# Gates by seven products in 42 of 48 quads, first products copied from bank to bank, and engine orders from a list scheduler

## The chip, the cores and the metric

The kernel runs on one core of one Trainium2 chip. The metric is the time of one execution on the device in microseconds, as the median of several runs. Before the change it is 533.65 us (three runs, 532.7 to 536.5). The profile shows one execution of 529.3 us from its first to its last instruction.

The core has five engines, each with its own instruction stream: TensorE (PE; PEld is its loading of weights) multiplies matrices and writes to PSUM, a memory of eight banks of 128 x 512 fp32; VectorE (DVE) works element by element; ScalarE (ACT) applies functions and copies; GpSimd (POOL) and SyncE (SP) here mostly start DMA transfers. [...]

## The reference

Attention in which keys and values are first projected from 1024 positions to 64, and then a feed-forward layer with a sigmoid gate. Inputs and output are fp32; the kernel computes its products in bf16.

```python
# attention: q, k, v are (8, 8, 1024, 64), E and F are (64, 1024)
k_proj = np.einsum('ks,bhsd->bhkd', E, k)
v_proj = np.einsum('ks,bhsd->bhkd', F, v)
scores = np.matmul(q, k_proj.transpose(0, 1, 3, 2)) / 8
attn = np.exp(scores - scores.max(-1, keepdims=True))
attn = attn / (attn.sum(-1, keepdims=True) + 1e-09)
x = np.matmul(attn, v_proj)            # then (8192, 512): heads side by side

# feed-forward: w_gate, w_val are (512, 1536), w_out is (1536, 512)
gate = 1.0 / (1.0 + np.exp(-(x @ w_gate)))
out = (gate * (x @ w_val)) @ w_out
```

## The kernel before

**The unit of work.** The 8 batches have 1024 rows of x each. Half a batch (512 rows) is a block, so there are 16 blocks. The hidden width of 1536 is cut into 12 pieces of 128. A quad is one third of a block: two pieces of the lower half of the hidden width and two of the upper half, for 512 rows. There are 3 quads a block, 6 a batch, 48 in all. Block 0 (three quads) is computed plainly while weights arrive; from quad 3 on the values use Strassen's scheme in Winograd's form: 7 products of half size in place of 8, with sums of operands beforehand and sums of products afterwards. The output product uses the same scheme from block 1 on. `vT`, `wT` hold sums of weights, `xS`, `hS` sums of the left operands.

**Gates**, one step for one piece: four matmuls of 512 columns into a PSUM bank, then a tanh on ScalarE (the sigmoid is written as a tanh of half the argument). `K` is the quad, `n` is 0 to 3.

```python
def g_step(K, n):
    ...
    bk = FF.take()
    for i in range(NI):                      # NI = 4
        mm_one(blk, m, i, "G", bk)           # 128x128 weights, 512 columns
    act(sg[:, n % 2, :], bank[bk][:, :], ..., func=AF.Tanh, scale=0.5)
    FF.append(bk)
```

**Values**, one quad: seven products of four matmuls of 256 columns, in two banks `a` and `c`. The first product is needed in two sums. It is copied to SBUF (`v_snap`) and added there to the second product (`v_add`). Products 2 and 6 and so on go on adding to bank `a`, which ScalarE copies at two points. `hidden` multiplies value and gate.

```python
def p1():
    held_v["a"] = a = FF.take()
    v_product(blk, q, a, "A11", "B11", start=True)
    v_snap(0, a)                                         # ACT: bank a -> SBUF

def p26():
    a = held_v["a"]
    held_v["c"] = c = FF.take()
    v_product(blk, q, c, "A12", "B21", start=True, stop=True)
    v_add(0, c)                                          # DVE: bank c + SBUF
    v_product(blk, q, a, "S2", "T2")
    v_snap(1, a)
    hidden(K, 0, 0, vsnap[0][:, :], [("vsnap", 0)])      # DVE: (tanh + 1) * value

def p57():  # S1 T1 into c, S3 T3 into a; v_snap(2, a); v_add(2, c)
def p4():   # A22 T4 into a; hidden from bank a; hidden from vsnap 2
def p3():   # S4 B22 into c; v_add(1, c); hidden from vsnap 1
```

**Output**, one block: `first_products` and `last_products` make seven products of 12 matmuls of 256 columns, with copies `keep_snap` (ACT) and sums `add_snap` (DVE) in the same manner. `s_sums` makes the sums of the left operands in VectorE, some split into a part of 4 and a part of 2 pieces.

**Attention** of batch b + 1 runs beside the feed-forward work of batch b. K and V are projected (16 matmuls), scores go through Exp, sums of the exponentials (denominators) are made by matmuls with a selection matrix, and the mixed values are copied unscaled to `xu`. The reciprocals are gathered by small DMAs and spread to all partitions by GpSimd; then VectorE multiplies:

```python
def spread(rnd):
    for j in range(4):
        n = 4 * rnd + j
        for c, parts in ((1, P), (0, 64)):
            pool(lambda e, ...: e.partition_broadcast(rb[0:parts, n, :], rrow[...], channels=parts), ...)

def x_half(r, g, bks):                                   # ACT: PSUM -> xu
    act(xu[:, n, :], bank[bks[g]][:, :], [], [("xu", n)], b=bks[g])

def mul(r, g, bk=None):                                  # DVE: xT = xu * rb
    y = rb[:, n, :] if bk is None else bank[bk][:, :]
    dve(lambda e: e.tensor_tensor(xT[...], xu[:, n, :]..., y..., ALU.mult), ...)
```

**The order** of each engine is written by hand: the quad's pieces are put in a row (`todo`), and other work is hung on positions in it.

```python
def quad_pieces(K, more):
    p1, p26, p57, p4, p3 = v_pieces(K)
    return [p1, lambda: g_step(K, 1), p26, lambda: g_step(K, 2), p57,
            lambda: g_step(K, 3), p4, lambda: g_step(K + 1, 0)], p3
...
on(2, 0, lambda: first_products(o0, first))              # quad 2, position 0
on(2, 2, lambda: last_products(o0))
on(ks, 0, n["scores"]); on(ks + 1, 0, n["mixed"]); on(3, 0, n["outputs"])
```

Four banks (`FF`) serve gates and values, four (`AA`) outputs and attention; a bank is taken from the head of its list and given back at the end.

Of the kernel before, what the change touches and what calls it, by code (L numbers as in the profile page):

```python
# [7 lines left out]
ALU = mybir.AluOpType  # L8
# [18 lines left out]

class Plan:
# [3 lines left out]
    def __init__(self):  # L32
        self.ops = []
        self.writers = {}
        self.readers = {}
        self.dma_count = {}

    def add(self, eng, fn, r=(), w=(), x=(), dma=None):
# [80 lines left out]
def bass_linformer_attn__then__ffn_glu_sigmoid_kernel(  # L119
# [18 lines left out]
    with contextlib.ExitStack() as es:  # L138
# [6 lines left out]
        wT = sbuf("wT", [P, 4, NF // 2, 256], BF16)  # L145
# [3 lines left out]
        def within(shape, dtype):  # L149
# [38 lines left out]
        rb = (  # L188
            KVs[:, :, :, :].rearrange("p w h c -> p (w h c)").bitcast(FP32)
            .rearrange("p (n c) -> p n c", n=8)  # L190
        )
# [6 lines left out]
        rrow = (  # L198
            eT[:, :, :].rearrange("p n c -> p (n c)").bitcast(FP32)
            .rearrange("p (i c) -> p i c", i=4)  # L200
        )
# [11 lines left out]
        snap = [EF[:, 0:512], EF[:, 512:1024], sbuf("snap2", [P, 512], FP32)[:, :]]  # L213
        vsnap = [sbuf(f"vsnap{i}", [P, 512], FP32) for i in range(3)]
        xS = [sbuf(f"xS{i}", [P, 4, 2, 256], BF16) for i in range(2)]
# [50 lines left out]
        def act(o, i, r, w, b=None, func=AF.Copy, scale=1.0):  # L266
            x = [] if b is None else [("bank", b)]
            return add("ACT", lambda e: e.activation(o, i, func, scale=scale), r=r, w=w, x=x)  # L268

        def dve(fn, r, w, b=None):  # L270
            x = [] if b is None else [("bank", b)]
            return add("DVE", fn, r=r, w=w, x=x)
# [8 lines left out]
        def load(o, i, w, sem, r=()):  # L281
            add("POOL", lambda e: e.dma_start(o, i), r=r, w=w, dma=sem)  # L282
# [487 lines left out]
        def keep_kd(bk):  # L770
# [8 lines left out]
                b=bk,  # L779
            )  # L780
# [11 lines left out]
        def vd_one(bk, g):  # L792
# [6 lines left out]
            )  # L799

        def attention(b):
# [44 lines left out]
            def rec(c):  # L846
# [5 lines left out]
                    b=bk,  # L852
                )
# [54 lines left out]
            def gather():  # L908
                for m in (0, 1, 4, 5, 2, 3, 6, 7):
                    half_, i = m // 4, m % 4  # L910
                    add(
                        "SP",
                        lambda e, m=m, i=i, half_=half_: e.dma_start(
                            rrow[::32, i, 256 * half_ : 256 * half_ + 256], rden[m::32, :]
                        ),
                        r=[("rden", c, R) for c in range(2) for R in range(2)],
                        w=[("rrow", i, half_)] + [("eT", 2 * i + x) for x in range(2)],
                        dma=f"rrow{m}",
                    )

            def spread(rnd):
                for j in range(4):
                    n = 4 * rnd + j
                    for c, parts in ((1, P), (0, 64)):
                        pool(
                            lambda e, n=n, i=2 * rnd + c, j=j, parts=parts: e.partition_broadcast(  # L926
                                rb[0:parts, n, :], rrow[32 * j : 32 * j + 1, i, :], channels=parts
                            ),
                            r=[("rrow", 2 * rnd + c, x) for x in range(2)]
                            + [("eT", 4 * rnd + 2 * c + x) for x in range(2)]  # L930
                            + ["q7"],
                            w=[("rb", n), ("KV", n // 4, n % 4 // 2)],
                        )

# [19 lines left out]
            def mul(r, g, bk=None):  # L954
                n = 2 * r + g
                y = rb[:, n, :] if bk is None else bank[bk][:, :]
# [7 lines left out]
                    [("xu", n)]  # L964
# [90 lines left out]
            def keep_kv(n):  # L1055
                if "kv" not in held:
                    return
# [770 lines left out]
```

The softmax here doesn't subtract the row's maximum and nothing guards it: scores larger than these inputs give would overflow.

## Time and profile before

| | busy us | share of 529.3 us | instructions |
|---|---|---|---|
| TensorE, matmuls | 515.5 | 97% | 4110 |
| TensorE, weight loads | 350.8 | 66% | 4173 |
| VectorE | 416.3 | 79% | 681 |
| ScalarE | 307.2 | 58% | 551 |
| GpSimd | 133.4 | 25% | 148 |

Busy shares say how full an engine is on average over the whole span, not what it waits for. Matmul times in the profile include the pipeline, so successive ones overlap: the mean of one 512-column gate matmul is 379 ns in the groups, though they start closer together than that; starts in the timeline give the true spacing. Some matmul records are missing (707 of 768 of the gate matmuls are there).

The costliest groups outside TensorE on the page (line, engine, operation, out<-in, shape, count | busy us, mean ns | idle time before, and what ended most of it):

```profile
L926 POOL PARTITION_BROADCAST KVs<-eT x96 | 96.8, 1035 | 243.5 <-PE pF L264 190.7
L268 ACT ACTIVATE sig<-pF 128x512 f32<-128x512 f32 x192 | 115.4, 601 | 49.3 <-PE pF L264 47.3
L1476 DVE TENSOR_TENSOR vsnap<-pF,vsnap 128x512 f32<-128x512 f32 x135 | 93.0, 689 | 39.7 <-PE pF L264 29.5
L958 DVE TENSOR_TENSOR xT<-xu,KVs 128x512 bf16<-128x512 f32 x48 | 47.4, 1023 | 1.2 <-POOL KVs L926 0.7
```

The names are those of the buffers: `pF` and `pA` are PSUM banks, `sig` a gate, `vsnap` a value's partial sum, `rb` lies in `KVs` and `rrow` in `eT`. ScalarE and VectorE idle mostly until TensorE has finished a product.

### The profile page before, as it was taken

What the parts mean: (1) busy time and instruction counts of PE and PEld (TensorE: products, weight loads), DVE (VectorE), ACT (ScalarE), POOL (GpSimd) and SP (SyncE); (2) the same over time, 40 slices, a digit from 0 to 9 for tenths busy, and PEclk for the clock granted to TensorE, in tenths of its full rate; (3) what the DMA queues carried; (4) which work ended last, traced back from release to release, by engine and by line L of the source; (5) the groups of instructions that cost most, each with busy time, mean ns of one, the idle gap of its engine ahead of it and who ended that gap; (6) DMA issues with size and microseconds to landing.
All of it is one profiled execution on the core that took longest, in us unless ns stands there. A gap on an engine that the chain in (4) does not pass through costs nothing.

```text
span 529.3 us, 10415 instructions
## 1 busy us (share of the span) xinstructions
PE 515.5 (97%) x4110; PEld 350.8 (66%) x4173; DVE 416.3 (79%) x681; ACT 307.2 (58%) x551; POOL 133.4 (25%) x148
## 2 busy tenths in 40 slices
PE   5999999999999999999999999999999999999997
PEld 4545646656857667585766767576685867677676
DVE  4549786788987788877988779877888788997855
ACT  2565753688385564946468474764838564554541
POOL 9310200106700085001920048100650009200000
PEclk9999999999999999999999999999999999999999
DMA  9999999994393255911589223962620020202022
GB/s 167 199 199 202 155 213 195 184 171 89 35 230 60 82 91 84 231 53 38 90 157 162 80 40 57 213 105 80 88 86 1 0 83 3 80 1 79 1 81 80
DMA packets 77154, 56.18 MB, mean 106 GB/s; under 512 B 34801, under 2 KB 69297, under 8 KB 77105
## 3 DMA queue, kind: packets, MB, share of 16 engines
q0 software_dynamic: 33984, 29.89, 36.6%
q1 hardware_dynamic: 43120, 25.63, 19.4%
q8 instruction: 32, 0.52, 0.4%
q14 instruction: 18, 0.14, 0.1%
HBM read 60.29 MB, written 16.78 MB: 146 GB/s over the span
## 4 chain that ended last, share of the span: by engine, by line
PE 90%; DMA 7%; issue 1%; POOL 1%; DVE 0%; ACT 0%; POOLq 0%
PE pF L264 59%; PE pA L264 31%; DMA wO<-in_moe_w_out_dram 2%; DMA qT<-Qb 2%; DMA KVs<-in_v_dram 2%; POOL KVs L282 0%; POOL Qb L282 0%; DVE rden L639 0%; DVE vsnap L1476 0%; ACT vsnap L268 0%; DVE ost L1338 0%; POOL quad L356 0%; POOLq L102 0%; POOLq L1813 0%
## 5 line engine op out<-in xcount | busy, mean ns | idle before, releaser
L264 PE MATMUL pF<-xT,wG 128*128 128x512 bf16 x707 | 186.8, 379 | 3.8 <-DMA wG<-in_moe_w_gate_dram 0.2
L926 POOL PARTITION_BROADCAST KVs<-eT x96 | 96.8, 1035 | 243.5 <-PE pF L264 190.7
L268 ACT ACTIVATE sig<-pF 128x512 f32<-128x512 f32 x192 | 115.4, 601 | 49.3 <-PE pF L264 47.3
L1476 DVE TENSOR_TENSOR vsnap<-pF,vsnap 128x512 f32<-128x512 f32 x135 | 93.0, 689 | 39.7 <-PE pF L264 29.5
L264 PEld LDWEIGHTS pF<-xT,wG 128*128 128x128 bf16 x768 | 74.2, 98 | 54.5 <-issue 1.7
L268 ACT ACTIVATE vsnap<-pF 128x512 f32<-128x512 f32 x135 | 80.7, 598 | 46.9 <-PE pF L264 42.4
L1457 DVE SCALAR_TENSOR_TENSOR hT<-sig,vsnap 128x512 bf16<-128x512 f32 x135 | 93.5, 693 | 6.2
L264 PE MATMUL pF<-xT,wV 128*128 128x256 bf16 (+1 forms) x408 | 66.9, 286 | 0.0
L264 PE MATMUL pA<-wO,hT 128*128 128x256 bf16 x534 | 63.4, 273 | 0.0
L264 PEld LDWEIGHTS pA<-wO,hT 128*128 128x128 bf16 x534 | 52.1, 98 | 6.6 <-DVE ost L1267 0.3
L264 PE MATMUL pF<-xS,wV 128*128 128x256 bf16 x360 | 54.1, 273 | 0.3
L264 PEld LDWEIGHTS pF<-xT,wV 128*128 128x128 bf16 x408 | 38.2, 98 | 23.9 <-issue 5.7
L264 PE MATMUL pF<-xS,vT 128*128 128x256 bf16 x360 | 54.0, 273 | 0.0
L264 PEld LDWEIGHTS pF<-xS,wV 128*128 128x128 bf16 x360 | 34.3, 98 | 25.6 <-DVE vsnap L1476 5.0
L958 DVE TENSOR_TENSOR xT<-xu,KVs 128x512 bf16<-128x512 f32 x48 | 47.4, 1023 | 1.2 <-POOL KVs L926 0.7
L268 ACT ACTIVATE EF<-pA 128x512 f32<-128x512 f32 x30 | 17.9, 597 | 46.9 <-PE pA L264 46.9
L264 PE MATMUL pA<-wT,hT 128*128 128x256 bf16 x360 | 44.2, 273 | 0.0
L264 PE MATMUL pA<-wT,hS 128*128 128x256 bf16 x360 | 41.7, 273 | 0.0
L264 PEld LDWEIGHTS pA<-wT,hT 128*128 128x128 bf16 x360 | 35.1, 98 | 7.4 <-ACT snap L268 0.3
L264 PEld LDWEIGHTS pA<-wT,hS 128*128 128x128 bf16 x360 | 35.1, 98 | 4.3 <-issue 0.2
L264 PEld LDWEIGHTS pF<-xS,vT 128*128 128x128 bf16 x360 | 35.2, 98 | 4.1
L1267 DVE SCALAR_TENSOR_TENSOR ost<-pA,EF 128x512 f32<-128x512 f32 x29 | 20.0, 688 | 19.8 <-PE pA L264 19.7
(113 smaller groups left out, 487.6 us busy)
## 6 DMA issues: line engine op xcount, KB each, us to landing
out_dram<-ost SPq DMA_DIRECT2D x60, 256.0 KB, 2.4
Qb<-in_q_dram POOLq DMA_DIRECT2D x7, 1024.0 KB, 20.5
KVs<-in_k_dram POOLq DMA_DIRECT2D x7, 1024.0 KB, 12.0
KVs<-in_v_dram POOLq DMA_DIRECT2D x7, 1024.0 KB, 16.2
wO<-in_moe_w_out_dram POOLq DMA_DIRECT2D x1, 1536.0 KB, 12.3
wG<-in_moe_w_gate_dram POOLq DMA_DIRECT2D x5, 256.0 KB, 17.9
wV<-in_moe_w_val_dram POOLq DMA_DIRECT2D x5, 256.0 KB, 18.5
KVs<-in_k_dram POOLq DMA_DIRECT2D x2, 512.0 KB, 7.8
```

Source lines behind the costliest of these rows:

```text
L264: return add("PE", lambda e: e.matmul(o, lhsT, rhs, **kw), r=r, x=[("bank", b)])
L268: return add("ACT", lambda e: e.activation(o, i, func, scale=scale), r=r, w=w, x=x)
L926: lambda e, n=n, i=2 * rnd + c, j=j, parts=parts: e.partition_broadcast(rb[0:parts, n, :], rrow[32 * j : 32 * j + 1, i, :], channels=parts),
L958: lambda e: e.tensor_tensor(xT[s][:, r, :, 256 * g : 256 * g + 256], xu[:, n, :].rearrange("p (f c) -> p f c", f=2), y.rearrange("p (f c) ...
L1267: lambda e: e.scalar_tensor_tensor(o, bank[bk][:, :].rearrange("p (j c) -> p j c", j=2), 0.5, snap[n].rearrange("p (j c) -> p j c", j=2), ...
L1457: lambda e: e.scalar_tensor_tensor(o, sg[:, :, cc], 1.0, x.rearrange("p (j c) -> p j c", j=2), ALU.add, ALU.mult,),
L1476: lambda e: e.tensor_tensor(o, bank[bk][:, :], o, ALU.add),
```

## The change

Three things change from batch 1 (quad 6) on; batch 0 keeps its way.

1. **Gates by seven products too.** 42 of 48 quads compute x @ w_gate as the values are computed: seven products of four 256-column matmuls (`g_chain`), in two banks, with `gT` for the sums of weights, made once by `gt_sums`. This is to spare one product in eight.
2. **The first product is copied from PSUM bank to PSUM bank** (`seed`). The second product then adds to it in the bank, and its addition on VectorE goes away. Values, gates and outputs all use it.
3. **The order of each engine comes from a list scheduler** (`arranged`), run when the program is built: tasks with assumed durations (`COST`), dependencies and target times (`goal`, with `PACE = 9.9` us a quad); an engine takes, among the tasks that are ready, the most urgent. Banks are fixed: two each for gates, values and outputs, two more for attention.

To make room in SBUF some buffers shrink. And the reciprocals go to DRAM and come back as broadcast loads into `xu` (`rd`, `rb`); VectorE multiplies straight from PSUM (`scaled`), so the copy to `xu` and the GpSimd broadcasts go. The third sum of x rows replaces A21 in place, and the output's sums are made for six pieces at once.

The diff, cut to its core:

```diff
+COST = {"PE": (0.0, 0.22), "ACT": (0.52, 0.12), "DVE": (0.63, 0.12), "SP": (0.1, 0.0), "POOL": (0.85, 0.0)}
+def arranged(tasks, free):
+    ...   # dependencies from the keys that tasks read and write; rank from goals
+        for e, some in ready.items():
+            first = max(now[e], min(t.at for t in some))
+            pick = min((t for t in some if t.at <= first + 1e-9), key=lambda t: (t.rank, t.n))
...
-        wT = sbuf("wT", [P, 4, NF // 2, 256], BF16)
+        wT = sbuf("wT", [P, 3, NF // 2, 256], BF16)
+        gT = sbuf("gT", [P, 3, 2, DFF // 2], BF16)
...
+        def seed(a, c):
+            add("ACT", lambda e: e.activation(bank[c][:, :], bank[a][:, :], AF.Copy, scale=1.0),
+                r=[("bank", c)], x=[("bank", a), ("bank", c)])
...
             def p1():
-                held_v["a"] = a = FF.take()
+                held_v["a"], held_v["c"] = a, c = FF.two()
                 v_product(blk, q, a, "A11", "B11", start=True)
-                v_snap(0, a)
+                seed(a, c)
             def p26():
-                v_product(blk, q, c, "A12", "B21", start=True, stop=True)
-                v_add(0, c)
+                v_product(blk, q, c, "A12", "B21", stop=True)
                 v_product(blk, q, a, "S2", "T2")
...
+        def g_chain(K, a, c, goals):
+            x_product(K, a, "A11", "B11", g0, True, True)
+            seed(a, c)
+            x_product(K, a, "S2", "T2", g1, True)
+            act(o12, bank[a][:, :], [], [k12], b=a)
+            x_product(K, c, "A12", "B21", g1 + 0.1, True)
+            tanh(o, bank[c][:, :], [], [k], b=c)
+            x_product(K, a, "S3", "T3", g2, True)
+            act(o22, bank[a][:, :], [], [k22], b=a)
+            x_product(K, c, "S1", "T1", g2 + 0.1, True, True)
+            plus_bank(o22, k22, c)
+            tanh(o22, o22, [k22], [k22])
+            x_product(K, a, "A22", "T4", g3, True)
+            tanh(o, bank[a][:, :], [], [k], b=a)
+            x_product(K, c, "S4", "B22", g4, True)
+            plus_bank(o12, k12, c)
+            tanh(o12, o12, [k12], [k12])
...      # v_chain: the same products for the values; o_chain: for the output
-            def gather(): ...      # 8 small DMAs
-            def spread(rnd): ...   # 8 partition_broadcast on GpSimd, twice
+            def spread():
+                add("SP", lambda e: e.dma_start(rd_v[b], rden[:, :]), ..., t=2.8)
+                for rnd in range(2):
+                    for c in range(2):
+                        for h in range(2):
+                            ...    # src = one row of rd_v for 64 partitions, 256 KB in SBUF
+                            add("SP", lambda e, ...: e.dma_start(rb[64 * c : 64 * c + 64, :, h, rnd, :], src), ..., t=4.0)
+            def scaled(r, g, bk):
+                dve(lambda e: e.tensor_tensor(xT[...], bank[bk][:, :]..., rb[:, j, :, rnd, :], ALU.mult), ...)
...
-            for u in range(6): ...  # todo, at, on(...): the order by hand
+        PACE = 9.9
+        GA, GC, VA, VC, OA, OC, XA, XB = A0, F0, A1, F1, A2, F2, A3, F3
+        for b in range(1, B):
+            for u in range(6):
+                K = 6 * b + u; t0 = when(K)
+                if u == 0: n["sc_visit"](t0 - 1.0, (0, 1), (GA, GC, XA, XB))
+                if u == 1: n["sc_visit"](t0 - 1.0, (2, 3), (GA, GC, XA, XB)); n["den_visit"](t0 + 6.0, XA)
+                if u == 3: n["xo_visit"](t0 - 1.0, (0, 1), (GA, GC, XA, XB))
+                if u == 4: n["xo_visit"](t0 - 1.0, (2, 3), (GA, GC, XA, XB)); ...   # and K, V of b + 2
+                g_chain(K, GA, GC, [t0 + PACE * x for x in (0.0, 0.2, 0.4, 0.6, 0.8)])
+                v_chain(K, VA, VC, [t0 + PACE * x for x in (0.55, 0.75, 0.95, 1.15, 1.35)])
+                if K % 3 == 2: ...  # o_chain(blk, OA, OC, ...), at the end final_chain
+        for t in arranged(tasks, {}):
+            for eng, fn, r, w, x, dma in t.calls:
+                add(eng, fn, r=r, w=w, x=x, dma=dma)
```

## The prediction

> **What bounds the kernel now.** I read the page first: busy shares, then the chain that ended last. A busy TensorE alone proves little, because its matmuls overlap in the records; the chain says whether anything else ever ends last.
>
> ```profile
> PE 515.5 (97%) x4110; PEld 350.8 (66%) x4173; DVE 416.3 (79%) x681; ACT 307.2 (58%) x551; POOL 133.4 (25%) x148
> PE 90%; DMA 7%; issue 1%; POOL 1%; DVE 0%; ACT 0%; POOLq 0%
> ```
>
> 90% of the chain is matmuls, and the DMA part lies in the first 70 us. So after the start the kernel is a queue of matmuls with nothing between them, and only fewer or cheaper matmuls can shorten it. The next view, busy time by stretches, gives one period of the steady part (columns: window and its length, busy time and count of each engine, granted clock, DMA share, GB/s). Output products of successive batches start at 257.83, 320.49, 383.15 us in the chain, so a batch takes 62.66 us.
>
> ```profile
> 257.83:320.49 62.66, 62.20 (x491) 43.19 (x497) 51.53 (x81) 38.49 (x70) 18.68 (x20) 1.00 0.52 102
> 320.49:383.15 62.66, 62.20 (x490) 43.18 (x497) 51.53 (x81) 38.49 (x70) 18.85 (x20) 1.00 0.56 104
> ```
>
> VectorE is at 51.5 of 62.66 us (82%), ScalarE at 38.5 (61%). Neither bounds, but VectorE has only 11 us in hand. The clock is full, so no reserve lies there. Now the matmul's own price, from TensorE's timeline (start, length, then the group):
>
> ```profile
> 276.18 0.60 PE L264 MATMUL pF<-xS,vT 128*128 128x256 bf16 x4
> 276.62 1.03 PE L264 MATMUL pF<-xT,wG 128*128 128x512 bf16 x4
> 277.48 0.60 PE L264 MATMUL pF<-xS,wV 128*128 128x256 bf16 x4
> 277.92 0.60 PE L264 MATMUL pF<-xS,vT 128*128 128x256 bf16 x4
> ...
> 304.11 0.62 PE L264 MATMUL pA<-eT,dsel 128*32 128x256 bf16 x16
> 304.67 0.41 PE L264 MATMUL pF<-eT,vpD 64*64 64x512 bf16 x4
> 304.90 0.39 PE L264 MATMUL pA<-eT,vpD 64*64 64x512 bf16 x4
> 305.22 1.92 PE L264 MATMUL pA<-KVs,EFT 128*64 128x512 bf16 x16
> 307.07 0.61 PE L264 MATMUL pF<-xT,wV 128*128 128x256 bf16 x4
> ```
>
> Lengths include the pipeline and overlap; starts are what counts. Four gate matmuls of 512 columns take 277.48 - 276.62 = 0.86 us, 0.2165 each when several such steps are averaged. Four of 256 columns take 0.436, so 0.109 each; a run of 60 in the chain takes 6.55 us, the same 0.109. Attention pieces: denominators 0.56, eight mixing matmuls 0.55, the K and V projection 1.85.
>
> [...]the trace has 216.5 and 109, [...]and splitting one matmul in two costs 2 ns. [...]the multiplications xT<-xu,KVs average 1.02 us beside the broadcasts and 0.65 us when two of them run clear of one.
>
> **The change, part by part.** *Gates by seven products.* Before, one quad of gates is 4 steps of 4 matmuls of 512 columns: 16 x 0.2165 = 3.46 us. After, it is 7 products of 4 matmuls of 256 columns: 28 x 0.109 = 3.05 us. Saved 0.41 us a quad, all of it on the path, since TensorE is the path. 42 quads x 0.412 = **17.3 us**.
>
> *Attention visits.* Before, scores and mixing come as 12 + 12 + 8 matmuls (0.78 + 0.77 + 0.55 us from starts); after, as four groups of eight, 4 x 0.55 = 2.20 us. Lost 0.1 us a batch, **0.6 us** over six batches.
>
> *ScalarE per batch.* Gates go from four tanh a quad to one seed copy, two snaps and four tanh: +3 x 6 = 18. Values stay at three. Output chains have one more (two per batch). The eight copies of the unscaled mixing result into xu go. Net 18 + 2 - 8 = 12, so 38.5 + 12 x 0.60 = 45.7 us of about 60: 76%, beside TensorE.
>
> *VectorE per batch.* Gates bring two additions a quad (12 x 0.689 = 8.3 us); the seed removes one addition a quad of values (-4.1) and one per output chain (-1.4); eight multiplications read PSUM, 0.68 in place of 1.02 (-2.7, the broadcasts on GpSimd are gone). Net 0.1 us: 51.6 of about 60, 86%. It moves from 82%, still below TensorE.
>
> *Reciprocals through DRAM.* One store and eight broadcast loads of 256 KB per batch replace 16 broadcasts on GpSimd. A 256 KB store lands in 2.4 us; at the 230 GB/s that the page's best slices reach, eight need 2.1 MB / 230 = 9 us. Only the first four are needed for the first mixing visit, which comes about two quads (20 us) after the denominators. Hidden, by this estimate.
>
> *Weight sums.* Four more VectorE operations of 1536 elements, 0.95 each = 3.8 us once, where batch 1 starts (about 85 us). The output chain of block 1 (9.2 us of matmuls) and first products that need no sum lie beside them. I charge **0.5 us**.
>
> *The order.* The period now holds 62.66 - 4.51 (attention) - 96 x 0.2165 - 336 x 0.109 = 0.75 us of idle, as in the windows (62.66 - 62.20 with records missing). After, the work is 504 x 0.109 + 4.61 = 59.5 us. A static order for every engine, made from assumed durations, meets queues that are fuller on ScalarE and VectorE. Bank chains have room: four products with a copy or addition behind each cost about 4 x (0.44 + 0.2 + 0.6) = 5.0 us of a quad's 9.9, where 0.2 is the gap seen from a product's end to its reader. I choose 0.25 to 0.3 us more idle a batch, **2 us** in seven.
>
> Sum: 533.65 - 17.3 + 0.6 + 0.5 + 2 = 519.5; the old order's own small waits may shrink a little, so I say **519.0 us**, 2.7% less.
>
> **The rivals.** *A: bank waits take the place of the matmuls saved.* For it: waits that already exist are exactly of this kind,
>
> ```profile
> PEld pF L264 <- ACT vsnap L268: 14.6, 44, 0.6
> PEld pF L264 <- DVE vsnap L1476: 6.6, 17, 0.5
> PEld pF L264 <- ACT sig L268: 2.9, 7, 0.4
> ```
>
> (waiter, releaser, total, times, longest), and the change doubles the number of products that wait on a copy. Against it: three chains with banks of their own are interleaved, so there is other work, and these are waits of weight loads, which run ahead. If each of 84 gate and value chains lost 0.15 us more, that is 13 us: **530 us**.
>
> *B: the broadcast loads are late and VectorE blocks in order.* For it: loads of Q land after 20.5 us at the median, on the same 16 DMA engines. Against it: the slack of about 20 us above, and a mean DMA share of 0.5. A delay of 4 us in six batches would be 24 us: **543 us**.
>
> *C: the scheduler removes nearly all idle.* Then only the arithmetic counts, 0.75 us a batch is won as well: 533.65 - 17.3 + 0.6 - 5 = **512 us**.
>
> **Range and chances.** C gives the lower end, 512; A, nearly in full, the upper, 529. The 2% line is at 523.0, 4 us above the middle, so A at a third of its size already crosses it. Faster by over 2%: 0.68; within 2%: 0.26, mostly A; slower by over 2%: 0.06, which takes B and A together.
>
> **What would show it.** Right: no 512-column gate matmuls after batch 1 starts, 256-column ones still 0.109 apart; a period near 60 us with TensorE busy all but 1 us; ScalarE near 46 and VectorE near 52 us per period; the scaling multiplications near 0.68; GpSimd with almost nothing but DMA issues. Wrong: waits of TensorE on seeds, snaps or additions that total over 10 us, VectorE waiting for the broadcast loads, or a hole in TensorE's slices near 85 us or at the end.

## The result and the profile after

The changed kernel takes **554.63 us** (median of four runs, 552.23 to 555.62) against 533.17 us (530.99 to 536.5) for the kernel before in the same series. The ratio is 1.0396, 95% interval 1.0350 to 1.0442: slower, where 519.0 us had been predicted.

From the page of the changed kernel: busy shares, TensorE's 40 slices, its granted clock, and the chain that ended last by engine and by line.

```profile
PE 513.7 (93%) x4677; PEld 403.8 (73%) x4677; DVE 406.2 (73%) x670; ACT 352.1 (64%) x644; POOL 37.0 (7%) x52
PE   5999995992999989999799979999999999999996
PEclk9999998996999989999899998999999999999999
PE 76%; DMA 17%; DVE 3%; SPq 2%; POOL 1%; issue 1%; ACT 0%; DVEq 0%; ACTq 0%; POOLq 0%
PE pA L372 44%; PE pF L372 32%; DMA xu<-rd 6%; DMA Qb<-in_q_dram 5%; DMA rd<-rden 3%; DMA KVs<-in_v_dram 2%; SPq L1145 2%; POOL KVs L390 1%; DMA qT<-Qb 1%; DVE xT L1158 1%; DVE rden L961 0%; DVE xT L799 0%; DVE hT L1262 0%; DVE hT L1784 0%; POOL Qb L390 0%
```

TensorE's busy time has fallen by only 1.8 us, and it is no longer the whole chain: 17% of it is transfers. The chain names them: the reciprocals on their way out (`rd<-rden`) and back (`xu<-rd`), and the load of Q. The slices show dips near 85, 125, 200, 262 and 328 us, and behind each the granted clock dips too.

Busy time by stretches (window and length; then busy time and count of TensorE, weight loads, VectorE, ScalarE, GpSimd; clock, DMA share, GB/s): batch 1, and one undisturbed period late in the span.

```profile
85.00:145.00 60.00, 42.58 (x366) 33.12 (x361) 34.20 (x54) 31.05 (x57) 3.51 (x4) 0.86 0.94 172
388.91:449.29 60.38, 60.38 (x570) 50.03 (x569) 49.59 (x78) 44.61 (x81) 0.00 (x0) 1.00 0.32 79
```

The second line is what the change was meant to give: 62.66 us a batch have become 60.38, with no idle time in TensorE. The first line is where it fails: 366 matmuls in 60 us instead of 570, a clock of 0.86, and DMA engines at 94%.

TensorE's timeline at two of the dips (start, length, group, idle before it and what ended it):

```profile
92.04 0.60 PE L372 MATMUL pA<-qT,kpD 64*64 64x512 bf16 x1 [6.13 <-issue]
135.79 1.03 PE L372 MATMUL pA<-xT,wG 128*128 128x256 bf16 x4 [10.34 <-DVE xT L1158]
136.61 1.06 PE L372 MATMUL pA<-xT,vT 128*128 128x256 bf16 x4
...
199.73 0.61 PE L372 MATMUL pA<-xT,wG 128*128 128x256 bf16 x4 [2.01 <-DVE xT L1158]
200.18 0.69 PE L372 MATMUL pA<-xT,vT 128*128 128x256 bf16 x4
200.92 1.04 PE L372 MATMUL pF<-xS,wV 128*128 128x256 bf16 x4
201.75 1.06 PE L372 MATMUL pA<-xS,gT 128*128 128x256 bf16 x4
202.60 1.06 PE L372 MATMUL pF<-xT,wG 128*128 128x256 bf16 x4
203.46 1.07 PE L372 MATMUL pA<-wO,hT 128*128 128x256 bf16 x6
204.37 0.60 PE L372 MATMUL pA<-xT,gT 128*128 128x256 bf16 x4
```

After the 10.34 us of idle, four matmuls of 256 columns take 136.61 - 135.79 = 0.82 us in place of 0.44. After the smaller wait at 199.73 the pace is right at first, then half from about 200.6 to 204, and right again at 204.37. The stretches before, in and after it (columns as above; the clock is the third number from the end) say why:

```profile
197.15:200.56 3.41, 1.40 (x14) 0.96 (x11) 1.58 (x3) 0.23 (x2) 0.00 (x0) 1.00 1.13 214
200.56:203.97 3.41, 3.36 (x17) 2.18 (x16) 3.41 (x7) 1.32 (x3) 0.00 (x0) 0.50 1.10 291
203.97:207.38 3.41, 3.41 (x33) 2.99 (x32) 2.26 (x4) 2.37 (x5) 0.00 (x0) 1.00 0.31 116
```

The granted clock is exactly half between 200.56 and 203.97. So a hole can cost twice: once as a wait, once as matmuls at half the clock.

**The account.** From starts of matmuls, a step between two of them counted as a hole where it is over 1 us: 6.51 + 1.33 us at the start of batch 1, 10.61 in it, 2.29, 4.08 and 3.62 in batches 2 to 4, together 28.4 us. (A last one of 1.02 us, in the final output, is left out.) In five stretches of half clock right behind the holes, doubled steps lose 9.4 us more. Some 40 single steps of 0.2 us stand elsewhere, most where the shape of the matmuls changes; the granted clock there is full, so they are not counted. The profiled span is 553.0 us, and 553.0 - 28.4 - 9.4 = 515.2. The span before, less seven times the 2.28 us by which a period became shorter, is 529.3 - 16.0 = 513.3. So the loss is accounted for to 2 us, by subtraction; the experiments have to show its causes.

**Who is waited for.** From the waits of the changed kernel (waiter, releaser, total, times, longest):

```profile
DVE xT L1158 <- DMA xu<-rd: 23.7, 4, 10.9
PEld pA L372 <- DVE xT L1158: 20.6, 4, 10.6
PE pA L372 <- DVE xT L1158: 19.5, 4, 10.3
DVE vsnap L1662 <- ACT vsnap L376: 13.9, 13, 1.9
```

The first three are one wait passed on. VectorE's scaling of the mixed values waits four times for the broadcast loads. Until it is done the mixed values fill the banks of the gates (`xo_visit` takes `GA` and `GC`), so TensorE's next gates wait for it. The fourth, the largest wait on a copy by number, is 13 short pieces of VectorE's own idle time; in the chain ScalarE, which makes the copies, has 0%. Why the loads are late is read in SyncE's queue (start, length of the row, operation; a row can hold waits):

```profile
88.73 33.33 SPq L853 DMA_TRANSPOSE qT<-Qb  x7
122.11 0.57 SPq L1128 DMA_DIRECT2D rd<-rden  x1
122.78 1.23 SPq L853 DMA_TRANSPOSE qT<-Qb  x1
124.15 8.73 SPq L1145 DMA_DIRECT2D xu<-rd  x8
```

VectorE's reciprocals ended at about 112.4 us, yet their store left at 122.11: it stood behind transposes of Q in SyncE's stream, the last of which waited for the load of Q of batch 3. The row of 33.33 us holds that wait: from 100 to 123 us SyncE's own waits name the load of Q with 10.9 us, and a single transpose takes 1.2 to 1.3 us. In batches 2 to 4 nothing holds the queue and the cause is another one, seen in the chain and in GpSimd's timeline:

```profile
122.11 2.02 DMA rd<-rden
184.18 6.45 DMA rd<-rden
248.52 6.92 DMA rd<-rden
314.30 1.97 DMA rd<-rden
318.39 11.82 DMA xu<-rd
```

```profile
182.29 0.87 POOL L390 DMA_DIRECT2D Qb<-in_q_dram  x1 [27.73 <-DMA qT<-Qb]
246.40 0.87 POOL L390 DMA_DIRECT2D Qb<-in_q_dram  x1 [26.48 <-DMA qT<-Qb]
313.77 0.88 POOL L390 DMA_DIRECT2D Qb<-in_q_dram  x1 [28.40 <-DMA qT<-Qb]
```

The same 128 KB store takes 2.0 us at 122 and 6.5 and 6.9 us at 184 and 249. There GpSimd had issued a load of Q of 1 MB at 182.29 and 246.40, 1.9 and 2.1 us earlier. At 314, with the load issued only 0.5 us earlier, the store is quick but the load of Q falls into the broadcasts: 11.8 us. The scheduler had been told 2.8 us for the store and 4.0 for a broadcast load; the 48 broadcast loads take 4.2 us at least, 7.6 at the median and 13.3 at most.

### The profile page after: what moved, and what is told of

It reads as the page before. It is cut to its first block, busy times and chain, and to the rows that moved or that the text cites. A ratio compares the mean times of both kernels' runs of the same rounds, so it can differ in the third digit from the quotient of the medians.

```text
span 553.0 us, 11355 instructions
## 1 busy us (share of the span) xinstructions
PE 513.7 (93%) x4677; PEld 403.8 (73%) x4677; DVE 406.2 (73%) x670; ACT 352.1 (64%) x644; POOL 37.0 (7%) x52
## 4 chain that ended last, share of the span: by engine, by line
PE 76%; DMA 17%; DVE 3%; SPq 2%; POOL 1%; issue 1%; ACT 0%; DVEq 0%; ACTq 0%; POOLq 0%
PE pA L372 44%; PE pF L372 32%; DMA xu<-rd 6%; DMA Qb<-in_q_dram 5%; DMA rd<-rden 3%; DMA KVs<-in_v_dram 2%; SPq L1145 2%; POOL KVs L390 1%; DMA qT<-Qb 1%; DVE xT L1158 1%; DVE rden L961 0%; DVE xT L799 0%; DVE hT L1262 0%; DVE hT L1784 0%; POOL Qb L390 0%
## 5 line engine op out<-in xcount | busy, mean ns | idle before, releaser
L376 ACT ACTIVATE sig<-pA 128x512 f32<-128x512 f32 x126 | 74.9, 595 | 55.4 <-PE pA L372 55.4
L1651 ACT ACTIVATE pF<-pA 128x512 f32<-128x512 f32 x99 | 58.1, 587 | 56.3 <-PE pA L372 30.1
L1662 DVE TENSOR_TENSOR vsnap<-pF,vsnap 128x512 f32<-128x512 f32 x90 | 61.9, 688 | 28.4 <-ACT vsnap L376 13.9
L1738 DVE TENSOR_TENSOR sig<-pF,sig 128x512 f32<-128x512 f32 x84 | 57.4, 683 | 23.3 <-PE pF L372 18.0
L372 PE MATMUL pF<-wO,hT 128*128 128x256 bf16 (+1 forms) x402 | 59.2, 286 | 0.0
L376 ACT ACTIVATE sig<-sig 128x512 f32<-128x512 f32 x84 | 52.9, 630 | 7.8 <-DVE sig L1738 7.1
L372 PE MATMUL pA<-xT,vT 128*128 128x256 bf16 x336 | 52.0, 279 | 0.0
L372 PE MATMUL pF<-xT,wG 128*128 128x256 bf16 (+1 forms) x264 | 51.1, 316 | 0.9 <-DVE hT L1262 0.8
L372 PE MATMUL pA<-xT,gT 128*128 128x256 bf16 x336 | 50.7, 274 | 0.3 <-ACT sig L376 0.3
L372 PE MATMUL pF<-xS,wG 128*128 128x256 bf16 x336 | 50.4, 273 | 0.0
L376 ACT ACTIVATE sig<-pF 128x512 f32<-128x512 f32 x66 | 39.3, 596 | 15.1 <-PE pF L372 13.2
L372 PEld LDWEIGHTS pF<-wO,hT 128*128 128x128 bf16 x402 | 38.5, 98 | 10.9 <-issue 1.2
L1784 DVE SCALAR_TENSOR_TENSOR hT<-sig,pF 128x512 bf16<-128x512 f32 x42 | 28.6, 682 | 11.1 <-PE pF L372 10.9
## 6 DMA issues: line engine op xcount, KB each, us to landing
Qb<-in_q_dram POOLq DMA_DIRECT2D x7, 1024.0 KB, 12.2
KVs<-in_k_dram POOLq DMA_DIRECT2D x7, 1024.0 KB, 10.6
wO<-in_moe_w_out_dram POOLq DMA_DIRECT2D x1, 1536.0 KB, 13.3
```

What stands on the lines that cost most here:

```text
L372: return add("PE", lambda e: e.matmul(o, lhsT, rhs, **kw), r=r, x=[("bank", b)])
L1651: lambda e: e.activation(bank[c][:, :], bank[a][:, :], AF.Copy, scale=1.0),
L1662: lambda e: e.tensor_tensor(o, bank[bk][:, :], o, ALU.add),
L1738: dve(lambda e: e.tensor_tensor(o, bank[bk][:, :], o, ALU.add), [key], [key], b=bk)
L1784: lambda e: e.scalar_tensor_tensor(o, sg.rearrange("p (j c) -> p j c", j=2), 1.0, x.rearrange("p (j c) -> p j c", j=2), ALU.add, ALU.mult,),
```

## The experiments

The theory: TensorE's holes come from transfers that are later than the scheduler was told, in part because they stand behind others in SyncE's queue, and the half clock multiplies them. The rivals: the seven-product gates or the bank-to-bank copies cost more than predicted; or the holes are the order's own. Every ratio is to the kernel before in the same series (532 us).

### 1 to 4: one cause at a time, on the changed kernel

**Transposes of Q only after the broadcasts** (`e1`):

```diff
-  r=[("Q", hf, r // 2) for hf in range(2)],                # transpose_q
+  r=[("Q", hf, r // 2) for hf in range(2)] + RB,           # RB: the keys of all 8 broadcasts
```

> TensorE's order is the changed kernel's, instruction for instruction; only SyncE's and GpSimd's orders differ: the transposes of Q for the batch after next wait until the broadcast loads of the reciprocals have landed, and so the next load of Q, which waits for these transposes, starts later too. Theory D (late reciprocals): the four holes before the scaling (10.6 + 2.3 + 4.1 + 3.6 us from start to start in the changed kernel's trace, with about 9 of its 12.6 us of half-clock matmuls) go; 554.6 - 20 - 9 = 526 us, and the hole at 85 us stays. Theory A (bank chains too tight for the order): the waits move to seeds, copies and additions, and the time stays above 545 us.

Measured 546.89 us, ratio 1.0276 (1.0252 to 1.0301): only 6 us less by the ratio (1.0396 for the unedited change). The hole of batch 1 fell from 10.6 to 3.2 us, the store leaving at 112.65. But four new holes of 2.3 to 3.6 us came in batches 2 to 5, with a wait that was not there before:

```profile
ACT ost L376 <- DMA out_dram<-ost: 19.0, 4, 5.3
```

ScalarE waits for a store of the output, which now stands in the same queue behind transposes that wait. So the expectation failed: the queue's head was moved, not removed. The time lies where the rival theory A had put it, above 545 us, but the waits are not on copies or additions, as that theory says.

**The load of Q only after the broadcasts** (`e2`): the same `RB` as a condition of `load_q`.

> Only the load of Q waits, for the broadcast loads of the batch before; the transposes keep their place ahead of the reciprocals' store. TensorE's order is unchanged. If the late reciprocals of batches 2 to 4 come from sharing the DMA engines with the load of Q, their store lands in about 2 us in place of 6.5 and their holes (2.3 + 4.1 + 3.6 us, with about 4 us of half clock) go, while the hole of batch 1 (10.6 us), which would come from SyncE's queue standing behind a transpose, stays or grows: about 541 us. If both have the queue order as cause, the time stays near 554. Theory A: near 554 too.

Measured 537.40 us, 1.0108 (1.0068 to 1.0149), as expected in kind and 4 us better: the hole of batch 1, expected to stay, shrank too. The holes of batches 2 to 4 are gone, their stores land in 1.7 to 2.4 us, and half clock costs 4.8 us in place of 9.4. Left are 6.2 + 1.3 us at the start and 7.5 in batch 1. This one edit takes the ratio from 1.0396 to 1.0108, 15 us. The collision of the load of Q with the reciprocals was the cause of the later holes.

**The scheduler told longer times** (`e3`): 24 us for the load of Q, 6.5 for the store, 10 for a broadcast. These lie near the long ones of the changed kernel and not at its medians (12.2, 2.0 and 7.6 us).

> Only three numbers that the scheduler assumes are changed to about what the changed kernel's trace shows: load of Q 24 us in place of 14, store of the reciprocals 6.5 in place of 2.8, each broadcast load 10 in place of 4. Theory D: the scheduler then puts the transposes behind the reciprocals by itself and moves other matmuls ahead of those that wait, so most of the 20 us of holes of batches 1 to 4 go: 525 to 532 us. Theory A: no gain, above 548.

Measured 549.14 us, 1.0292 (1.0239 to 1.0345). This is near the rival's outcome (above 548, waits on copies), though 5 us under the unedited change. The holes at the late broadcasts went, and others came in each batch, of about 1.06 and 1.5 to 3.2 us, with TensorE waiting on the bank-to-bank copies. (Its profile is of a run longer than the median, so it is used for the places only.) Longer assumed times alone do not make a good order: the orders of TensorE, ScalarE and VectorE shift as well.

**Transposed Q assumed 8 us after the start** (`e4`): `t.at = 8.0` for tasks that read `qT`, the scores.

> Only the start is changed: the scheduler is told that the transposed Q of batch 2 is there 8 us after the start of batch 1's work, where it assumed 0. TensorE then begins with the output products of block 1. The hole at 85 us (6.5 + 1.3 us) and its half-clock stretch (about 3.5 us) go: about 543 us; the holes of batches 1 to 4 stay about as they are. If the hole came from the weight sums on VectorE in place of Q, TensorE still waits there and the time stays near 554.

Measured 561.51 us, 1.0561 (1.0496 to 1.0626). The start's hole shrank to 2.84 + 1.94 + 0.8 us. But the whole order of SyncE moved, and both sets of transposes went ahead of the reciprocals:

```profile
93.23 11.28 SPq L855 DMA_TRANSPOSE qT<-Qb  x4
108.04 3.14 SPq L1418 DMA_DIRECT2D out_dram<-ost  x4
125.38 6.49 SPq L855 DMA_TRANSPOSE qT<-Qb  x4
131.93 0.57 SPq L1130 DMA_DIRECT2D rd<-rden  x1
```

The store now leaves at 131.93 and the hole of batch 1 is 18.6 us. So the late Q made a part of the start's hole, and taking that part away was bought with the next hole: the time is 18 us above the expectation.

### 5: both conditions, the second in batch 1 only

`e5` is `e2` with `transpose_q(RB if b == 1 else ())`.

> As e2_q_load_after, and in batch 1 alone the transposes of Q for batch 3 wait until the broadcast loads have landed, so that the reciprocals' store no longer stands behind a transpose in SyncE's queue. If the queue order makes the hole of batch 1, its store goes out at about 112.6 us in place of 120.9 and the hole shrinks from 7.5 us to about 2 to 3 (the loads of K, V and Q for batch 3 are still in flight): 537.4 - 5 - 2 of half clock = about 530 us. If the hole comes from the shared DMA engines alone, it stays: 537.

Measured 530.92 us, 0.9978 (0.9961 to 0.9995), as expected. The store leaves at once when VectorE's reciprocals are done (111.61):

```profile
87.98 5.37 SPq L854 DMA_TRANSPOSE qT<-Qb  x4
111.64 0.33 SPq L1129 DMA_DIRECT2D rd<-rden  x1
```

Batch 1's hole is 2.4 us, the periods are 60.40 us, half clock costs 3.6. Two conditions on transfers bring the ratio from 1.0396 to 0.9978, which is 22 us. In the traces of `e1`, `e2` and `e5` TensorE, ScalarE and VectorE each run the instructions of the changed kernel in the same order from batch 1 on. So neither the seven products, nor the bank-to-bank copies, nor the compute order can be the cause of these 22 us. That settles the main cause.

### 6 to 10: moving the attention visits by a quad, and what the arithmetic is worth there

**Batch 1's visits one quad later** (`e6`: `e2` with `a = u - int(b == 1)` in the conditions of the visits, and the target of batch 1's K and V projection 4 us earlier within its quad).

> As e2_q_load_after, and in batch 1 alone the attention visits come one quad later, as in the hand-written order, so that TensorE starts with output, gate and value products and Q of batch 2 has 10 us more to arrive. No wait is left that the theory of late transfers knows: the holes at 86 us (6.2 + 1.3) and of batch 1 (7.5) and the rest of the half clock (7.6 us) go: 537.4 - 15 - 7.6 = about 515 us, 3.5% under the kernel before. Then the count of matmuls was right and the transfers alone made the loss. If products seeded and snapped in this order cost more than counted, the time stays above 525.

Measured 535.68 us, 1.0069 (1.0035 to 1.0102), a miss. The start's hole fell from 7.5 to 2.8 us, but SyncE's queue held transposes from 88.60 to 121.0 us, the store left at 122.17, the hole of batch 1 is 7.9 us, and one of 4.2 came at 156, where the transposed keys of the projection are late.

**The same with plain gates** (`e7`: `g_chain` replaced by four groups of four 512-column matmuls and a tanh each, without `gT`).

> As e6_visits_later, but the gates of all quads are computed plainly again, four matmuls of 512 columns per 128 of the hidden width, in the same two banks; scheduler, seeds for values and outputs, and the way of the reciprocals stay. It leaves out no part of the computation. If 0.412 us a quad is what the seven products give, it is 17 us over e6_visits_later, at about 532 us, as the kernel before: the scheduler by itself gives nothing and costs nothing. If the scheduler's order were itself worth something, it would be below 527.

Measured 551.23 us, 1.0378 (1.0354 to 1.0401): 15.6 us above `e6`, near the 17.3 of the arithmetic; the absolute expectation, which rested on that of `e6`, failed with it.

**All visits one quad later** (`e8`: `e5` with `a = u - 1`, the K and V projections' targets 2 us earlier within their quads, and tasks that read the output weights from 3 us on).

> e5_queue_order (Q's load after the broadcast loads, batch 1's transposes behind them) with every attention visit of every batch one quad later, so that the visits have room in batch 1 and the next batch finds its projected keys, and with the scheduler told that the output weights' sums are ready 3 us after its start, so that TensorE begins with gates and values. e5_queue_order's holes are 6.7 + 1.3 us at 85 us and 2.4 us in batch 1, with 6.8 us of half clock. If these are all late transfers: 530.9 - 10 - 6.8 = about 514 us, 3.4% under the kernel before, and a period of 60.4 us. If something in the new order costs as well, above 522.

Measured 563.22 us, 1.0561 (1.0533 to 1.0588), the largest miss. Every batch from the second on has a hole of 4 to 5 us, and the waits name the stores again, 35.5 us in all:

```profile
ACT ost L378 <- DMA out_dram<-ost: 35.5, 5, 8.0
```

**On `e8`: first products through SBUF as before** (`e9`, no seed) and **plain gates** (`e10`).

> As e8_visits_later_all, but from batch 1 on the first products are copied to SBUF and added on VectorE, as in the kernel before, in place of the copy from bank to bank; the last output chain keeps its copy. 14 more additions a batch on VectorE, 8.5 us at 0.61 us from start to start: 49.6 becomes 58 of 60.4 us, and six more waits on VectorE in the gates' chains. If the copy between banks is what keeps VectorE out of the way, the period grows: 3 to 10 us over e8_visits_later_all. If it changes nothing but a reserve, within 2 us.

> As e8_visits_later_all, but all gates computed plainly, four matmuls of 512 columns a step. No part of the computation is left out. The seven products save 0.412 us in 42 quads by the prediction's count: 17 us over e8_visits_later_all, so about 531 us, the time of the kernel before; a little more if two banks are too few for plain gates, each of which holds a bank for its tanh.

Measured 542.51 us (1.0185; 1.0164 to 1.0206) and 557.44 us (1.0467; 1.0446 to 1.0489). Both are faster than `e8`, by 21 and 6 us, though each takes a saving away. Their holes are smaller (none over 3.0 us in `e9`), with another order. On a base with such holes the parts cannot be priced: an order's accident is larger than either part.

### 11 and 12: attention in banks of its own

The visits of two pieces use the gates' banks `GA, GC` too. `e11` is `e5` with single pieces in `XA, XB` alone and transposed Q assumed at 8 us; `e12` does so in batch 1 only.

```diff
-  n["sc_visit"](t0 - 1.0, (0, 1), (GA, GC, XA, XB))
+  for r, g in ((2 * u, 3.0), (2 * u + 1, 6.0)):            # e12: if b == 1
+      n["sc_visit"](t0 + g - 4.0 * u, (r,), (XA, XB))
```

> e5_queue_order with every attention visit of all batches in the two attention banks alone, one head pair at a time and mixing a few us later, so that a late reciprocal no longer holds the gates' banks; and the scheduler told that Q of batch 2 arrives 8 us after its start, so that TensorE begins with products. Eight visits of four matmuls in place of four of eight cost about 0.5 us a batch, 3 us in all. Theory of late transfers: e5_queue_order's holes (6.7 + 1.3 + 2.4 us) and its 6.8 us of half clock shrink to about 3 us at the start: 530.9 - 14 + 3 = about 520 us. If VectorE, which works in order, still stands before a late broadcast load, everything behind it stands too, and the time is above 530.

> As e11_visits_in_own_banks, but in batch 1 alone; later batches as in e5_queue_order, which ran without holes there with a period of 60.4 us. Without the 0.5 us a batch for smaller visits: about 517 us if the start and batch 1 run clean, 3% under the kernel before. If batch 1's reciprocals come too late again, because the products ahead of them no longer lose 8 us at the start, a hole of 3 to 5 us stays in batch 1: 522 us.

Measured 532.40 us (1.0012; 1.0000 to 1.0024) and **527.88 us** (0.9928; 0.9913 to 0.9943). `e12` is the fastest version: 0.7% under the kernel before, clear of the noise but far from the 2.7% predicted. Its stretches, the first batch 1 and the others two steady periods, and the wait that is left in batch 1:

```profile
85.00:145.40 60.40, 53.62 (x467) 41.36 (x464) 44.13 (x70) 38.36 (x70) 5.26 (x6) 0.94 0.94 169
188.66:249.07 60.41, 60.41 (x571) 50.00 (x568) 49.52 (x79) 44.59 (x82) 2.62 (x3) 1.00 0.74 136
249.07:309.47 60.40, 60.40 (x570) 50.02 (x568) 49.57 (x79) 44.59 (x82) 2.62 (x3) 1.00 0.78 150
```

```profile
125.06 0.69 DVE L1161 TENSOR_TENSOR xT<-pA,xu 128x512 bf16<-128x512 f32 x1 [5.60 <-DMA xu<-rd]
```

467 matmuls in batch 1's stretch in place of 366. Holes of 2.84 us at the start and 2.98 + 0.59 + 1.81 in batch 1 remain, the latter with 2.9 us of half clock behind them. So the second outcome named, a hole of 3 to 5 us in batch 1, came, at a time 6 us above the 522 expected for it. The store took 5.7 us there, beside the loads of K and V of batch 3.

### 13 and 14: the loads of batch 3 moved, on `e12`

`e13` issues the loads of K and V of batch 3 early (at 87 us in place of 98); `e14` does so with V, and issues K and Q only after the broadcasts.

> e12_own_banks_batch_1 with K and V of batch 3 loaded as soon as K and V of batch 2 are used, at about 86 us in place of 98, so that they are through before the reciprocals go out and come back. If these loads make batch 1's reciprocals late: the store lands in about 2 us in place of 5.7, the broadcasts earlier by 4 us and more, batch 1's hole (about 5 us in all) and its half-clock stretch (most of 6.5 us) go: 527.9 - 5 - 5 = about 518 us. If the loads then make the transposes of Q for batch 2 late instead, a hole appears at 96 us and the time stays at 526 or above.

> e12_own_banks_batch_1 with the load of K of batch 3, and so that of Q behind it, held back until the broadcast loads have landed; V goes early. The other way to keep them apart: batch 1's hole goes as in e13_loads_of_3_early, about 518 us, unless K or the transposed Q now comes too late for the end of batch 1 (140 us) or the start of batch 2 (146 us), which would show as a hole there and 522 to 530 us.

Measured 533.83 us (1.0044; 1.0029 to 1.0059) and 533.20 us (1.0016; 1.0001 to 1.0031). In each the hole that was aimed at shrank or went (1.8 us are left in `e13`). In `e14` the store lands in 1.7 us and nothing waits for a broadcast in batch 1. And in each a larger one came elsewhere: in `e13` 6.7 us at 96.5, because the transposes of Q take 17 us beside those loads, and another of 3.7 at 170.5; in `e14` 6.2 us at 149.7, where the transposed keys of batch 3 land at 155.83, behind the transposes of Q in SyncE's queue. These are the second outcomes that the expectations named.

### 15 and 16: each part taken back, on `e12`

`e15` has plain gates (the edit of `e7`); `e16` takes first products through SBUF as before (the edit of `e9`).

> e12_own_banks_batch_1 with plain gates, 16 matmuls of 512 columns a quad in place of 28 of 256. No part is left out. By the count 0.412 us in 42 quads: 17 us slower than e12_own_banks_batch_1, about 545 us if holes stay alike; the period goes from 60.4 to about 62.9 us.

> e12_own_banks_batch_1 with first products copied to SBUF and added on VectorE from batch 1 on, as before the change. VectorE gets 8.5 us a batch more, 49.6 to 58 of 60.4 us. If the bank-to-bank copy is needed to keep VectorE off the path, the period grows by 1 us or more: 535 us or above. If not, within 2 us of 527.9.

**Plain gates:** 540.80 us (1.0163; 1.0133 to 1.0193), 12.9 us more than `e12`. The total is not a clean price: `e15` happens to lack `e12`'s 5.4 us of holes in batch 1 and the 2.9 us of half clock behind them, and has holes of its own of 0.8 to 2.1 us. A period without holes is:

```profile
378.40:441.06 62.66, 62.29 (x491) 43.42 (x497) 42.43 (x67) 36.16 (x63) 0.00 (x0) 1.00 0.30 75
```

62.66 us, to the hundredth what the hand-written order took before, against 60.40 with seven products. So seven products are worth 2.26 us a batch, 2.26 x 7 = 15.8 us in all, and the rest of the change neither gives nor costs anything in such a period.

**No seed:** 534.45 us (1.0042; 1.0024 to 1.0060), 6.6 us more than `e12`. VectorE rises from 49.6 us a batch, counted from one batch's denominators to the next's, to between 57.4 and 59.6. One stretch, longer than a batch of `e12`:

```profile
250.00:314.88 64.88, 62.36 (x570) 50.74 (x568) 58.76 (x95) 43.96 (x81) 2.62 (x3) 0.97 0.76 144
```

Holes of 1.3 to 3.5 us come that `e12` lacks. The copy from bank to bank takes 14 operations a batch (92 - 78) from the fuller engine, and the base with it is the faster one. That it would be so in any order is not shown: on `e8` taking it away made the kernel faster.

### 17 and 18: the hole of batch 1 avoided by moving the mixing

On `e12`, the K and V projection of batch 3 takes the place of the first mixing visit of batch 1, and the four visits come some 12 us later (`e17`); `e18` also delays the sums of the output weights to 3 us. This leaves part of the computation changed: the projected values share one buffer, so batch 2 is mixed with the values of batch 3. The operations and their number are the same, but the mixing now also waits for that projection.

> The version with own banks (527.9 us) still holds three gaps of TensorE in batch 1 at 122.8 to 128.2 us, 5.4 us together, and 2.99 us of half clock behind them, because the first mixing visit comes at 117.8 us and the reciprocals' broadcast lands at 125. Here only the places of batch 1's attention pieces change: the K and V projection of batch 3 takes the place of the first mixing visit (its loads land at about 115.5 us), and the four mixing visits come some 12 us later. Theory (late transfers and the half clock behind them are the loss): 527.9 - 5.0 - 3.0 = 520 us, gaps over 0.6 us of TensorE after 85 us only the one of 2.8 us at the start. Rival (the delay only moves to the next transfer, as in the two versions with the loads of batch 3 shifted): a new gap of 3 us or more in batch 1 or 2, and 525 us or more.

> As the one before, and the scheduler is told that the sums of the output weights can start 3 us after batch 1's start, so TensorE is given gates and values first, in place of the output product that waits 2.84 us for the in-place sum. Theory: 517 us, no gap over 1 us of TensorE after 85 us except the last one before the end. Rival: the changed start gives all later orders another shape, so new gaps of 2 to 5 us in the batches, as when this was done before with all visits one quad later (563 us): above 523 us.

Measured 531.98 us (0.9991; 0.9972 to 1.0009) and 531.38 us (0.9986; 0.9969 to 1.0003): the rival's outcome. The wait for the broadcasts is gone, and ScalarE waits for output stores instead, which stand in SyncE's queue behind transposes (`e17`, ScalarE's timeline):

```profile
136.32 0.60 ACT L378 ACTIVATE ost<-pF 128x512 f32<-128x512 f32 x1 [4.98 <-DMA out_dram<-ost]
...
170.96 0.60 ACT L378 ACTIVATE ost<-pF 128x512 f32<-128x512 f32 x1 [5.89 <-DMA out_dram<-ost]
```

TensorE has holes of 3.4 us at 134 and 5.1 us at 167 in their place; `e18` has 1.6 and 4.5 us there, and 2.3 and 3.0 us in the start.

## Why the prediction was wrong, step by step

**Gates by seven products, 17.3 us, less 2 us for 0.25 to 0.3 us more idle a batch: right.** The undisturbed period went from 62.66 to 60.38 us, and the comparison of `e12` with `e15` isolates 2.26 us a batch, 15.8 us in all. That is what is left after the idle that the shorter products bring, so it stands against 17.3 - 2 = 15.3. The matmuls still start 0.109 us apart.

**Attention visits, 0.6 us: in line with the period.** The period predicted is 59.5 + 0.75 + 0.3 = 60.5 us; measured 60.38.

**ScalarE 45.7 and VectorE 51.6 us a batch: right** within 1.1 and 2.0 us (44.6 and 49.6). The scaling takes 0.68 us as predicted. (It had taken 0.68 to 0.69 clear of a broadcast before, too; the 0.65 read there is half of a row of two that overlap.)

**Rival A, bank waits: did not come** in the changed kernel. The chain gives ScalarE 0%, the undisturbed period has no idle time, and TensorE's long waits are the ones passed on from a transfer. Bank waits do appear in `e3`, whose order was made for slower transfers.

**Weight sums, 0.5 us: the step fell short.** At the start of batch 1 the "first products that need no sum" were to lie beside the sums. The scheduler put the scores first instead: it begins at time 0 with all engines free and transposed Q there, and TensorE waited 6.5 + 1.3 us for it. With the scores moved, 2.8 us are left (`e6`, `e12`). In `e12` the in-place sum of the output weights ends at 87.68, ScalarE's copy of the projected values of batch 2 at 87.93, and the profile names the copy:

```profile
88.07 0.82 PE L374 MATMUL pA<-wO,hT 128*128 128x256 bf16 x6 [2.46 <-ACT vpD L378]
```

In `e8` and `e18`, where gates and values come first, 2.3 us stay, with TensorE waiting for a bank-to-bank copy that stands behind the same copies on ScalarE. So the sums are not all of what is left; how much is theirs stays open.

**Reciprocals through DRAM, "Hidden, by this estimate": the step that failed.** Its volume was right; the slack, the cost and the free path were not.

The slack was put at 20 us, two quads from the denominators to the mixing. By the diff's own targets it is less: denominators at 6.0 us into quad 1, mixing 1.0 us ahead of quad 3, so 2 x 9.9 - 7.0 = 12.8 us. Batch 5, undisturbed, has 14.0 us:

```profile
378.35 0.62 PE L372 MATMUL pA<-eT,dsel 128*32 128x256 bf16 x16
392.33 0.40 PE L372 MATMUL pA<-eT,vpD 64*64 64x512 bf16 x2
```

The cost was put at 2.4 us for the store and 9 for the eight loads. In batch 5, with no load of Q beside them, the reciprocals ended at 381.02, the store landed at 382.75, the fourth load at 391.89 and the eighth at 396.82: 14.1 us for the eight. That leaves 0.4 us ahead of the mixing at 392.33. So the path was barely hidden at best, and a delay shows soon.

Delays came in two ways. In batch 1 the store left 10 us late, because it stood in SyncE's stream behind the row of transposes from 88.73 to 122.06 (`e1`, with the transposes behind the broadcasts, cuts the hole to 3.2 us). In batches 2 to 4 the load of Q stood beside the transfers; the store then took up to 6.9 us and the loads up to 12.9 (`e2` removes these holes). Two signs that the prediction had named as wrong came with it: VectorE waiting for the broadcast loads, 23.7 us in all, and (from the late Q) a hole near 85 us. Rival B named this mechanism at 4 us a batch. It was set aside on this slack and on the mean DMA share of 0.5, but a mean over the period says nothing of the stretch in which the transfer runs: in batch 1 the share is 0.94.

**A term was missing altogether: half clock.** 9.4 us of the loss are matmuls at twice the pitch behind holes. At 202.60, with a granted clock of 0.50, four matmuls of 256 columns take 203.46 - 202.60 = 0.86 us in place of 0.44. The stretches of half clock in batches 1 to 4 last 3.41, 6.83 or 10.24 us, and their starts (91.33, 128.88, 200.56, 265.41, 330.26) lie whole multiples of 3.413 us apart. TensorE need not have been idle for all of the 3.41 us ahead of one: ahead of 200.56 it was busy for 1.40 us, and the hole was 2.29 us from start to start. A prediction that priced this hole at its length alone would be 1.4 us short.

In numbers: 519.0 us predicted; of the holes' 28.4 us only 0.5 were in the sum, and of the 9.4 us of half clock none. 519.0 + 27.9 + 9.4 = 556.3, which is 1.7 us above the measured 554.6; this rest was not traced.

**What stays open.** Subtraction says that the order without holes would have a span of about 515 us, some 517 us as a time: `e5` (528.3 - 10.3 - 3.6 = 514.4) and `e12` (526.2 - 8.2 - 2.9 = 515.1) give the same as the changed kernel (515.2). That is within 2 us of the 519.0 predicted. But no version reached it: the best is 527.9 us. Each removal of `e12`'s holes (`e13`, `e14`, `e17`, `e18`) let another transfer be the late one, so this time is argued, not shown. That two conditions on transfers are worth 22 us (`e5`) is shown.

## What to carry to other kernels

A static order is only as good as the transfer times it was made with. Before a small store or broadcast is put on the path between two engines, look at the queue that issues it (what ahead of it waits for data?) and at the large loads beside it, in that stretch and not in the mean. Work the slack out from the order itself, from the instruction that starts the path to the one that needs its end, and not in round units of work. When TensorE has no idle time, price a new wait at its length plus the half clock that may follow it: 1.4 to 2.9 us behind the changed kernel's holes of 2.29 to 10.61 us. And when parts of a change are to be priced, compare undisturbed periods: `e8`, which is `e5` with the attention work moved by a quad, took 32 us more.

## What the runs showed of the hardware that was not expected

- A hole of 2.29 us between matmul starts was followed by 3.41 us at half clock (14 steps doubled, 1.4 us lost), beginning 0.8 us after work had resumed. A hole of 2.84 us at the start of batch 1 in `e12` had no such stretch behind it. On the grid of 3.413 us on which the starts of half clock lie, the first hole falls into one stretch, in which TensorE was busy for 1.40 us; the second is cut by a border at 86.39 (placed from `e12`'s half clock at 127.35, twelve times 3.413 us later), with about 2.6 and 1.7 us busy on its two sides. That this is the reason is not shown: in the changed kernel 1.41 us busy in 84.50 to 87.92 was followed by a stretch at full clock, though one without a matmul.
- The same 128 KB store to DRAM landed in 1.97 to 2.02 us or in 6.45 to 6.92 us, the latter with a 1 MB load issued about 2 us ahead of it on GpSimd's queue.
- ScalarE's copy from PSUM bank to PSUM bank takes 587 ns for 512 columns, against 595 to SBUF, both means of the changed kernel's page: the bank as a target costs nothing extra.
